# A first MLP product from three one-pass float32r products of 12-bit parts, in place of float32 half products of a seven-product scheme

## The chip, the cores and the metric

The kernel runs on one core of one Trainium2 chip. The time is device microseconds from the start to the end of one execution. The kernel before takes 355.83 us, the median of three runs (355.64 to 357.01). TensorE (PE) multiplies matrices and writes to PSUM; VectorE (DVE), ScalarE (ACT) and GpSimd (POOL) do the elementwise work; SyncE (SP) starts most of the transfers. Each engine has its own queue and works through it in the order of the program.

## What is computed

Two blocks follow each other. The first is a Mamba-2 state-space layer over 4 batches, 8 heads, 768 tokens, with heads 32 wide and a state of 16. The second is an MLP with a hard-swish on 3072 tokens of width 256, with 2048 hidden columns:

```
x = attn_out.transpose(0, 2, 1, 3).reshape(B * S, H * D)   # 3072 x 256
h = x @ w_in                                               # 256 -> 2048
relu6 = np.clip(h + 3.0, 0.0, 6.0)
g = h * relu6 / 6.0
return (g @ w_out).astype(np.float32)                      # 2048 -> 256
```

The weights arrive as float64, so the kernel decodes them to float32 from their bits.

## The kernel before

The sequence is cut into six chunks (`NC`) of 128 positions. A chunk holds 128 positions of all 4 batches, so 512 tokens (`TB`). For each chunk the state-space layer makes `yT`, which is 256 features (two tiles of 128, index `j`) by 512 tokens. The first MLP product turns it into 16 tiles `gT` (index `f`) of 128 hidden columns by 512 tokens, and the second MLP product turns those into the output. The program is software-pipelined by hand: the state-space work of chunk `c = k + 1` stands inside the second MLP product of chunk `k`, and loads stand one chunk further ahead. Nothing is reordered; the order in which the Python code emits instructions is the order in each engine's queue.

**Weights.** Each weight matrix comes in four parts (0 to 3 are `w_in`, 4 to 7 `w_out`), 1 MB each. `decode(i)` is a generator with five steps, and `weights(i, n)` takes n of them. Step 1: ACT copies the top 16 bits (L198). Step 2: DVE takes exponent, sign and high mantissa bits (L215, L217, L201). Step 3: ACT, first half of the exponent (L221). Step 4: ACT, second half (L223), and DVE the full mantissa (L205). Step 5: DVE joins sign and exponent (L228) and multiplies (L236), which finishes 128 x 1024 weights. The dictionary `weave` says after which `f` of chunk 0 each step is emitted. Parts 0 and 1 are decoded before chunk 0's MLP, parts 2 to 5 within its first product, 6 and 7 at the beginning of its second.

**First product, chunk 0.** `mlp_in(0, f)` multiplies in plain float32: two products of 128 x 128 weights by 512 tokens per `f` (L616), then `ramp` on ACT (L694: relu of h/6 + 1/2) and `times_ramp` on DVE (L699: the smaller of that and 1, times h). Its results go through four PSUM banks, f0 to f3.

**First product, chunks 1 to 5.** A seven-product scheme on 2 x 2 blocks of halves (features by token halves, hidden columns in even and odd tiles): for each pair `s` of hidden tiles, `lead`, `early`, `middle` and `last` issue seven products of 128 x 128 weights by 256 tokens (all at L658, in `half_product`), where a direct product would take eight. Its sums of weights are made once by `in_weight_sums` (L640), its sums of `yT` for each chunk by `sum_y` (L655, right after `keep`), and partial results are copied and added by ACT (L673, L680) and DVE (L674, L686, L687) between the products. `ramp` and `times_ramp` follow for each of the two tiles.

**Second product.** For chunk 0, `first_out` (L713): 128 products by four quarters `i` of the hidden columns and four batches `b`; quarter `i` needs part `4 + i` of the weights and the gT tiles 4i to 4i + 3. For chunks 1 to 4, `wide_units` (L836), and for chunk 5, `out_units` (L772), again in a seven-product scheme; POOL makes its sums of `gT` (`g_sums`, L758, four operations for every four tiles) and DVE its sums of weights (`weight_sums`, L740). The next chunk's `lead` for its first tiles is emitted near the end: before the last two products of `first_out`, or at unit 12 of `wide_units`.

**State-space work.** `scores`, `multiply`, `renew`, `mix` and `keep` (L527 to L608) for the next chunk stand inside the second product; `keep` copies the result into `yT` on ACT. `conceal` (POOL, L158), `decay` (ACT, L385) and `ends` (POOL, L396) prepare the chunk after that.

Of the kernel before, what the change touches and what calls it, by code (L numbers as in the profile page):

```python
# [8 lines left out]
FP32 = mybir.dt.float32  # L9
U32 = mybir.dt.uint32  # L10
# [10 lines left out]
def kernel(  # L21
# [34 lines left out]
    NQ = NH // 2  # L56
    HU = NH // 2
# [57 lines left out]
    def load_x(c):  # L115
        sl = slice(c * P, (c + 1) * P)
        xts[c] = loads.tile([P, NB * NH, D], FP32, name="xt")
        nc.sync.dma_start(out=xts[c], in_=x[:, :, sl, :].rearrange("b h s d -> s (b h) d"))

    w_in = const.tile([P, NK, DF], FP32, name="w_in")  # L120
    w_sum = const.tile([P, NF // 2, P], FP32, name="w_sum")
# [50 lines left out]
    nc.vector.memset(half, 0.5)  # L172
    bias_hi = const.tile([P, 1], FP32, name="bias_hi")
# [12 lines left out]

    def decode(i):
# [7 lines left out]
        s = att.tile([P, n], U16, name="ws")  # L195
        e = att.tile([P, n], U16, name="we")
# [33 lines left out]
        if i < NP:  # L230
            dst = w_in[:, :, i * FP * P:(i + 1) * FP * P]
            m, e = (t.rearrange("p (k f) -> p k f", k=NK) for t in (m, e))
        else:
            dst = w_out[:, (i - NP) * FP:(i - NP + 1) * FP, :]
            m, e = (t.rearrange("p (k f) -> p k f", k=FP) for t in (m, e))
# [8 lines left out]
    picks = const.tile([P, G * N], BF16, name="picks")  # L244
# [77 lines left out]

    yTs, states, mids, bTs, bss, tmps = {}, {}, {}, {}, {}, {}
# [67 lines left out]
    def ends(c, b):  # L391

        if b == 0:
            bss[c] = att.tile([P, G, N], FP32, name="bs")
        hs = slice(b * NH, b * NH + NH)
        nc.gpsimd.tensor_tensor(  # L396
            out=bss[c][:, hs], in0=Bs[c][:, hs],
            in1=Ls[c][:, b, :, HT - 1:HT].to_broadcast([P, NH, N]), op=ALU.mult)
# [174 lines left out]
    def renew(c):  # L573

        states[c] = att.tile([P, NB, 2 * D], FP32, name="state")
        later = att.tile([P, NB, 2 * D], FP32, name="later", bufs=1)
        nc.vector.tensor_tensor(
            out=later, in0=mids[c], in1=etos[c][:, :, P - 1:P].to_broadcast([P, NB, 2 * D]),
            op=ALU.mult)
        new_state(states[c], adds[c], later)  # L580
# [22 lines left out]
    def keep(c):  # L603

        yTs[c] = att.tile([P, NK, NB, P], FP32, name="yT")
# [7 lines left out]
    def mlp_in(k, f):  # L613
        h = ps.tile([P, NK, 2 * P], FP32, name="h", tag=f"f{f % 4}")
        for j in range(NK):
            nc.tensor.matmul(  # L616
                out=h.rearrange("p r i -> p (r i)"), lhsT=w_in[:, j, f * P:(f + 1) * P],
# [11 lines left out]
    wi = w_in.rearrange("p k (j e c) -> p k e j c", e=2, c=P)  # L629
    in_sums, y_sums, evens, odds, parts_of = {}, {}, {}, {}, {}  # L630

    def in_weight_sums():
        for h in range(2):
            js = slice(h * NJ // 2, (h + 1) * NJ // 2)
            a11, a12, a21, a22 = (wi[:, k, e, js] for e in range(2) for k in range(2))
            s1, s2 = (att.tile([P, NJ // 2, P], FP32, name="w_sum", tag=t) for t in ("ws", "we"))
            s4 = w_sum[:, js]
            for o, p_, q_, op in ((s1, a21, a22, ALU.add), (s2, s1, a11, ALU.subtract),
                                  (s4, a12, s2, ALU.subtract), (a21, a11, a21, ALU.subtract)):
                nc.vector.tensor_tensor(out=o, in0=p_, in1=q_, op=op)  # L640
            for n, t in ((1, s1), (2, s2), (3, a21), (4, s4)):
                in_sums.setdefault(n, []).extend(t[:, i] for i in range(NJ // 2))
            yield

    def y_half(k, j, r):
        return yTs[k][:, j, 2 * r:2 * r + 2].rearrange("p b i -> p (b i)")

    def sum_y(k):
        ts = att.tile([P, 3, 2 * P], FP32, name="ts", bufs=1)
        t1, t2, t4 = (ts[:, i] for i in range(3))  # L650
        t3 = y_half(k, 0, 1)
        y_sums[k] = {1: t1, 2: t2, 3: t3, 4: t4}
        for o, p_, q_ in ((t1, t3, y_half(k, 0, 0)), (t3, y_half(k, 1, 1), t3),
                          (t2, y_half(k, 1, 1), t1), (t4, y_half(k, 1, 0), t2)):
            nc.vector.tensor_tensor(out=o, in0=p_, in1=q_, op=ALU.subtract)  # L655

    def half_product(bank, r, lhsT, rhs, start=False):
        nc.tensor.matmul(  # L658
            out=bank[:, r], lhsT=lhsT, rhs=rhs, start=start, stop=True, skip_group_check=True)

    def lead(k, s):

        (pool, tag), (pool_e, tag_e) = (
            ((ps, "f0"), (ps, "f2")), ((ps, "f1"), (ps, "f3")),
            ((ps_y, "y0"), (ps_y, "y1")))[s % 3]
        odds[k, s] = odd = pool.tile([P, 2, 2 * P], FP32, name="odd", tag=tag)
        evens[k, s] = even = pool_e.tile([P, 2, 2 * P], FP32, name="even", tag=tag_e)
        parts_of[k, s] = up = ffn.tile([P, 2, 2 * P], FP32, name="up", bufs=2)  # L670
        half_product(odd, 1, wi[:, 0, 0, s], y_half(k, 0, 0), start=True)
        half_product(odd, 0, in_sums[3][s], y_sums[k][3])
        nc.scalar.copy(out=even, in_=odd[:, 1:2].to_broadcast([P, 2, 2 * P]))  # L673
        nc.vector.tensor_copy(out=up[:, 1], in_=odd[:, 0])  # L674

    def early(k, s):
        even = evens[k, s]
        half_product(even, 0, wi[:, 1, 0, s], y_half(k, 1, 0))
        half_product(even, 1, in_sums[2][s], y_sums[k][2])
        nc.scalar.copy(out=parts_of[k, s][:, 0], in_=even[:, 1])  # L680

    def middle(k, s):
        even, odd, up = evens[k, s], odds[k, s], parts_of[k, s]
        half_product(odd, 0, wi[:, 1, 1, s], y_sums[k][4])
        half_product(even, 1, in_sums[1][s], y_sums[k][1])
        nc.vector.tensor_tensor(out=odd[:, 0], in0=odd[:, 0], in1=up[:, 0], op=ALU.add)  # L686
        nc.vector.tensor_tensor(out=odd[:, 1], in0=even[:, 1], in1=up[:, 1], op=ALU.add)  # L687

    def last(k, s):
        half_product(evens[k, s], 1, in_sums[4][s], y_half(k, 1, 1))  # L690
# [12 lines left out]
    def first_out(b, i, c):  # L703
# [6 lines left out]
        for f in range(i * FP, (i + 1) * FP):  # L710
            if b == NB - 1 and f == NF - 2:
                lead(c, 0)
            nc.tensor.matmul(  # L713
                out=o[:, b % 2], lhsT=gTs[0][:, f, b * P:(b + 1) * P], rhs=w_out[:, f],
                start=(f == 0 and b % 2 == 0), stop=True, skip_group_check=True)
        if i == NP - 1 and b % 2:
            ob = ffn.tile([P, 2, DM], FP32, name="ob", bufs=2)
# [11 lines left out]
    def weight_sums():  # L729


        t3 = const.tile([P, NJ, P], FP32, name="t3")
# [27 lines left out]
    def out_units(k):  # L760
# [15 lines left out]
        for t in range(2):  # L776
# [9 lines left out]
            if t == 0:  # L786
                unit(oa, 0, quarter(0, 0, 0), w4[:, 0, 0], rest)
                unit(oa, 3, quarter(0, 0, 1), w4[:, 0, 0], rest)
                x1 = ffn.tile([P, 2, P], FP32, name="x1")
# [6 lines left out]
            res = ffn.tile([P, 5, P], FP32, name="res", bufs=2)  # L796
# [7 lines left out]
            u = ffn.tile([P, 2, P], FP32, name="u", bufs=2)  # L804
# [108 lines left out]
    def results(c, parts=range(2)):  # L913
        mix(c, parts)
        keep(c)
        sum_y(c)
# [4 lines left out]

    def load(c):
        load_bc(c)
        load_x(c)
# [60 lines left out]
    load(1)  # L985


    weave = {}
    for i in range(2, NP + 2):
        for j in range(5):  # L990
            weave.setdefault(4 * i - 8 + j, []).append(i)
    weave[NF - 1].append(NP + 2)
    for k in range(NC):
        gTs[k] = ffn.tile([P, NF, TB], FP32, name="gT")
        c, ahead = k + 1, k + 2
        if k == 0:
            for f in range(NF):
                mlp_in(k, f)
                for i in weave.get(f, []):
                    weights(i, 1)  # L1000
                if f in (6, 8):
                    diff_exp(c, f // 2 - 3)
            load(ahead)
# [3 lines left out]
            sums, sums_in = weight_sums(), in_weight_sums()  # L1007
            for i in range(NP):
                for b in range(NB):
                    first_out(b, i, c)  # L1010
                    if (i, b) == (0, 0):
                        weights(NP + 3, 1)
                        weights(NP + 2, 1)
                        weights(NP + 3, 3)
                        rows(ahead)
                    elif (i, b) == (1, 0):
                        next(sums_in)
                        next(sums_in)
# [16 lines left out]
                    elif (i, b) == (3, 1):  # L1035
                        results(c)
                        next(sums)
                        decay_ends(ahead, 3)
                    elif (i, b) == (3, 3):
# [3 lines left out]
        for s in range(NJ):  # L1043
            early(k, s)
            if s == 0:
                if ahead < NC:
                    load(ahead)
                if c < NC:
                    carry(c)
            if s < NJ - 1:  # L1050
                lead(k, s + 1)
            if s:
                last(k, s - 1)
                ramp(k, 2 * s - 2, evens[k, s - 1])
            middle(k, s)
            if s:
                times_ramp(k, 2 * s - 2, evens[k, s - 1])
            ramp(k, 2 * s + 1, odds[k, s])
            times_ramp(k, 2 * s + 1, odds[k, s])
            if s in (1, 3) and ahead < NC:  # L1060
                conceal(ahead, s // 2)
            if s in (3, 5) and c < TURN:
                turn(c, s // 4)
            if s in (2, 4, 6):
                g_sums(k, s - 2)
        for i, _ in enumerate((wide_units if c < NC else out_units)(k)):
            if i == 0:
                s = NJ - 1
                last(k, s)
                ramp(k, 2 * s, evens[k, s])  # L1070
                times_ramp(k, 2 * s, evens[k, s])
                g_sums(k, s - 1)
                if k == 1:
                    next(sums)
            if c < NC:
# [11 lines left out]
                if i == (7 if c == TURN else 6):  # L1087
                    results(c, (1,) if c == TURN else range(2))
                    if ahead < NC:
                        from_start(ahead)  # L1090
# [4 lines left out]
                if i == 12:  # L1095
                    lead(c, 0)

# [29 lines left out]
```

## Time and profile before

| view | value |
|---|---|
| median of the runs shown | 355.83 us |
| the profiled execution's span | 353.6 us |
| first product of chunk 0 on PE (L616) | 22.8 to 50.3 us, 64 records |
| second product of chunk 0, with the state-space work of chunk 1 | 50.3 to 83.0 us |
| chunk 1 (from its first `lead` to the next chunk's) | 83.0 to 137.5 us |
| chunks 2, 3, 4 | 53.9, 53.6 and 54.0 us |
| chunk 5 | 299.0 to 353.6 us |
| DVE multiply that finishes weight parts 2, 3, 4, 5, 6, 7 (L236), start | 33.84, 41.34, 48.35, 54.76, 60.68, 63.68 us |

The profile covers one execution. "Busy" counts the time in which an engine has at least one instruction; PE records overlap, since matmuls are pipelined, so the distance from start to start is the time that one costs in a stream. A float32 product of 128 x 128 weights leaves two MATMUL records and two weight-load records. "PEclk" is the clock granted to TensorE.

### The profile page before, as it was taken

What the parts mean: (1) busy time and instruction counts of PE and PEld (TensorE: products, weight loads), DVE (VectorE), ACT (ScalarE), POOL (GpSimd) and SP (SyncE); (2) the same over time, 40 slices, a digit from 0 to 9 for tenths busy, and PEclk for the clock granted to TensorE, in tenths of its full rate; (3) what the DMA queues carried; (4) which work ended last, traced back from release to release, by engine and by line L of the source; (5) the groups of instructions that cost most, each with busy time, mean ns of one, the idle gap of its engine ahead of it and who ended that gap; (6) DMA issues with size and microseconds to landing.
All of it is one profiled execution on the core that took longest, in us unless ns stands there. A gap on an engine that the chain in (4) does not pass through costs nothing.

```text
span 353.6 us, 8557 instructions
## 1 busy us (share of the span) xinstructions
PE 343.7 (97%) x3488; PEld 281.9 (80%) x3488; DVE 227.4 (64%) x426; ACT 178.7 (51%) x394; POOL 138.0 (39%) x139
## 2 busy tenths in 40 slices
PE   6699999999999999999999999999999999999996
PEld 2454458888887888888888888888888888888996
DVE  6689999975797437786437787436687322688111
ACT  4768887258764741665641575551575011466100
POOL 3300000362498621099612099710078600068700
PEclk9999999999999999999999999999999999999999
DMA  8999969502925052256034256001200001200000
GB/s 168 178 335 162 272 157 122 128 2 78 164 55 66 4 125 51 35 70 81 2 72 97 36 67 91 4 4 18 34 9 1 4 3 20 34 8 2 0 32 30
DMA packets 91607, 24.92 MB, mean 70 GB/s; under 512 B 84208, under 2 KB 87952, under 8 KB 91056
## 3 DMA queue, kind: packets, MB, share of 16 engines
q1 hardware_dynamic: 87184, 23.06, 35.7%
q10 hardware_dynamic: 4384, 1.31, 1.7%
q8 instruction: 27, 0.44, 0.5%
q14 instruction: 12, 0.10, 0.1%
HBM read 21.07 MB, written 3.29 MB: 69 GB/s over the span
## 4 chain that ended last, share of the span: by engine, by line
PE 91%; DVE 3%; DMA 3%; ACT 1%; SPq 1%; issue 1%; DVEq 0%; ACTq 0%
PE even L658 18%; PE odd L658 13%; PE wb L836 12%; PE wc L836 8%; PE o L713 8%; PE h L616 8%; PE wa L836 8%; PE oa L772 4%; PE ob L772 4%; PE y L594 3%; PE y L500 2%; PE cb L527 2%; DMA raw<-in_moe_w_in_dram 2%; PE y L539 1%; DMA pairs<-in_C_dram 1%; SPq L100 1%
## 5 line engine op out<-in xcount | busy, mean ns | idle before, releaser
L758 POOL TENSOR_TENSOR s<-gT 128x512 f32<-128x512 f32 x20 | 26.3, 1317 | 86.0 <-DVE gT L699 86.0
L658 PE MATMUL even<-ts,w_sum 128*128 128x256 f32 x160 | 48.2, 383 | 0.0
L694 ACT ACTIVATE gT<-odd,half 128x512 f32<-128x512 f32 x40 | 27.5, 688 | 34.9 <-DVE odd L687 34.9
L658 PE MATMUL odd<-yT,w_in 128*128 128x256 f32 x160 | 41.1, 379 | 0.0
L673 ACT COPY even<-odd 128x512 f32<-128x512 f32 x40 | 23.0, 576 | 27.7 <-PE odd L658 25.5
L658 PEld LDWEIGHTS even<-ts,w_sum 128*128 128x128 f32 x160 | 29.9, 190 | 5.3 <-ACT up L680 1.5
L699 DVE SCALAR_TENSOR_TENSOR gT<-gT,odd 128x512 f32<-128x512 f32 x40 | 27.5, 688 | 9.9 <-ACT gT L694 9.9
L658 PEld LDWEIGHTS odd<-yT,w_in 128*128 128x128 f32 x160 | 30.4, 190 | 4.1
L385 ACT ACTIVATE L<-L,cum_n 128x64 f32<-128x64 f32 x128 | 31.5, 340 | 0.0
L836 PE MATMUL wb<-s,w_out 128*128 128x256 f32 x128 | 30.7, 382 | 0.0
L694 ACT ACTIVATE gT<-even,half 128x512 f32<-128x512 f32 x40 | 27.8, 695 | 4.4 <-PE even L658 4.4
L699 DVE SCALAR_TENSOR_TENSOR gT<-gT,even 128x512 f32<-128x512 f32 x40 | 27.2, 679 | 4.4 <-ACT gT L694 4.4
L713 PE MATMUL o<-w_out,gT 128*128 128x256 f32 x128 | 28.7, 381 | 0.0
L616 PE MATMUL h<-yT,w_in 128*128 128x512 f32 x64 | 27.7, 594 | 0.0
L674 DVE COPY up<-odd 128x256 f32<-128x256 f32 x40 | 16.9, 423 | 15.8 <-ACT even L673 15.1
L713 PEld LDWEIGHTS o<-w_out,gT 128*128 128x128 f32 x128 | 24.1, 190 | 3.7 <-issue 0.5
L403 POOL TENSOR_TENSOR tmp<-state,eto 128x256 f32<-128x256 f32 x5 | 3.4, 684 | 60.4 <-DMA eto<-cum_e 51.1
L836 PEld LDWEIGHTS wb<-s,w_out 128*128 128x128 f32 x128 | 24.0, 190 | 3.4
L758 POOL TENSOR_TENSOR s<-s,gT 128x512 f32<-128x512 f32 x20 | 25.5, 1273 | 1.6
L758 POOL TENSOR_TENSOR gT<-gT 128x512 f32<-128x512 f32 x20 | 25.4, 1272 | 0.0
L758 POOL TENSOR_TENSOR s<-gT,s 128x512 f32<-128x512 f32 x20 | 25.4, 1270 | 0.0
L658 PE MATMUL even<-yT,w_sum 128*128 128x256 f32 x80 | 24.4, 387 | 0.2
(150 smaller groups left out, 657.9 us busy)
## 6 DMA issues: line engine op xcount, KB each, us to landing
raw<-in_moe_w_out_dram SPq DMA_DIRECT2D x4, 1024.0 KB
L<-cum_d SPq DMA_DIRECT2D x8, 512.0 KB
xt<-in_x_dram SPq DMA_DIRECT2D x6, 512.0 KB
raw<-in_moe_w_in_dram SPq DMA_DIRECT2D x3, 1024.0 KB
out_dram<-back SPq DMA_DIRECT2D x128, 16.0 KB
eto<-cum_e SPq DMA_DIRECT2D x20, 64.0 KB
B<-in_B_dram SPq DMA_DIRECT2D x5, 256.0 KB
raw<-in_moe_w_in_dram ACTq DMA_DIRECT2D x1, 1024.0 KB
```

Source lines behind the costliest of these rows:

```text
L385: nc.scalar.activation(Ls[c][:, b, h], Ls[c][:, b, h], AF.Exp, bias=cum_n[:, c, g:g + 1])
L594: nc.tensor.matmul(out=ys[c][a, u][d0:d0 + D, b], lhsT=xt[rows, b * NH + h], rhs=Ls[c][rows, b, h], start=(b == 0 and a >= min(c, 1)), sto ...
L616: nc.tensor.matmul(out=h.rearrange("p r i -> p (r i)"), lhsT=w_in[:, j, f * P:(f + 1) * P], rhs=yTs[k][:, j].rearrange("p b i -> p (b i)") ...
L658: nc.tensor.matmul(out=bank[:, r], lhsT=lhsT, rhs=rhs, start=start, stop=True, skip_group_check=True)
L673: nc.scalar.copy(out=even, in_=odd[:, 1:2].to_broadcast([P, 2, 2 * P]))
L674: nc.vector.tensor_copy(out=up[:, 1], in_=odd[:, 0])
L694: nc.scalar.activation(gTs[k][:, f], h.rearrange("p r i -> p (r i)"), AF.Relu, bias=half, scale=1.0 / 6.0)
L699: nc.vector.scalar_tensor_tensor(out=g, in0=g, scalar=1.0, in1=h.rearrange("p r i -> p (r i)"), op0=ALU.min, op1=ALU.mult)
L713: nc.tensor.matmul(out=o[:, b % 2], lhsT=gTs[0][:, f, b * P:(b + 1) * P], rhs=w_out[:, f], start=(f == 0 and b % 2 == 0), stop=True, skip_ ...
L758: nc.gpsimd.tensor_tensor(out=o, in0=p_, in1=q_, op=op)
L772: nc.tensor.matmul(out=bank[:, slot], lhsT=lhs[:, j], rhs=rhs[:, j], start=(clear and j == 0), stop=True, skip_group_check=True)
L836: nc.tensor.matmul(out=bank[:, slot], lhsT=lhs[:, j], rhs=rhs[:, j], start=(clear and j == 0), stop=True, skip_group_check=True)
```

## The change

`w_in` is no longer kept as one float32 tensor. Each weight and each element of `yT` is split into a high part (the value times 1 - 2^-13, rounded to the 12 significant bits of float32r by the write), and a low part (what is left, which the weights' split scales by 2^12), and a third array `gap` holds the difference of the two scaled parts. The product is then (gap x gap), scaled in PSUM by -2^-12/(1 + 2^-12), plus high x high, plus low x low: three products of float32r operands, each of 128 x 128 weights by 512 tokens and over two feature tiles, so six matmuls for each hidden tile. The factor 1 + 2^-12 that remains is taken up by the constants of the activation (`half_up`, `UP`).

- `lead(k, f)` issues the two gap matmuls and the scaling of the PSUM bank (ACT for even `f` and for all of chunk 0, DVE for odd `f` otherwise); `follow(k, f)` issues the other four matmuls, the relu on ACT and the multiply on DVE. `lead` runs two tiles ahead, over six banks.
- `split_y(k)` splits `yT` (one ACT and two DVE operations of 128 x 1024); it stands in `results` where `sum_y` stood, and for chunk 0 ahead of `mlp_in(0, 2)`.
- `split_w(i)` splits weight part i in three steps (ACT and POOL; ACT; DVE or POOL), placed by `part`.
- In chunk 0 the tiles 0 to 7 still go through `mlp_in` in float32, tiles 8 to 15 through `lead` and `follow`. Parts 0 and 1 of `w_in` are decoded into float32 scratch tiles, parts 2 and 3 in place. The steps of parts 2 and 3 now fall on f = 0 to 3 and 4 to 7.
- `in_weight_sums`, `sum_y`, `half_product`, `early`, `middle` and `last` are gone.
- To make room in SBUF, `xt` and `bs` have one buffer instead of two, and `load_x` of the chunk ahead moves from the head of the first product to behind `results`; scratch tiles share buffers (`later`, `x1`, `u`, `ob`, `res`, `picks`, `t3`).

```diff
+    w_high, w_low, w_gap = (
+        const.tile([P, NK, DF], FP32R, name=n) for n in ("w_high", "w_low", "w_gap"))
...
+    highs, lows, gaps, hs = {}, {}, {}, {}
+
+    def split_w(i, engine):
+
+        w = first_in[i]
+        high, low, gap = (t[:, :, i * FP * P:(i + 1) * FP * P] for t in (w_high, w_low, w_gap))
+        nc.scalar.mul(high, w, CUT)
+        nc.gpsimd.tensor_tensor(out=low, in0=w, in1=high, op=ALU.subtract)
+        yield
+        nc.scalar.mul(low, low, 1.0 / Z)
+        yield
+        engine.tensor_tensor(out=gap, in0=high, in1=low, op=ALU.subtract)
+        yield
+
+    def split_y(k):
+
+        y = yTs[k].rearrange("p k b i -> p (k b i)")
+        high, low = (att.tile([P, NK * TB], FP32R, name=n, tag="y", bufs=3) for n in ("high", "low"))
+        nc.scalar.mul(high, y, CUT)
+        nc.vector.tensor_tensor(out=low, in0=y, in1=high, op=ALU.subtract)
+        gap = att.tile([P, NK * TB], FP32R, name="gap", **Y_GAP[min(k, 1)])
+        nc.vector.scalar_tensor_tensor(
+            out=gap, in0=low, scalar=-1.0 / Z, in1=high, op0=ALU.mult, op1=ALU.add)
...
+    def in_product(h, w, y, f, start=False):
+        for j in range(NK):
+            nc.tensor.matmul(
+                out=h, lhsT=w[:, j, f * P:(f + 1) * P], rhs=y[:, j],
+                start=(start and j == 0), stop=True, skip_group_check=True)
+
+    def lead(k, f):
...
+        pool, tag = ((ps, "f0"), (ps, "f1"), (ps, "f2"), (ps, "f3"), (ps_y, "y0"),
+                     (ps_y, "y1"))[f % 6]
+        hs[k, f] = h = pool.tile([P, TB], FP32, name="h3", tag=tag)
+        in_product(h, w_gap, gaps[k], f, start=True)
+        if k and f % 2:
+            nc.vector.tensor_scalar(
+                out=h, in0=h, scalar1=-Z / UP, scalar2=None, op0=ALU.mult)
+        else:
+            nc.scalar.mul(h, h, -Z / UP)
+
+    def follow(k, f):
+        h = hs.pop((k, f))
+        in_product(h, w_high, highs[k], f)
+        in_product(h, w_low, lows[k], f)
+        g = gTs[k][:, f]
+        nc.scalar.activation(g, h, AF.Relu, bias=half_up, scale=UP * UP / 6.0)
+        nc.vector.scalar_tensor_tensor(
+            out=g, in0=g, scalar=UP, in1=h, op0=ALU.min, op1=ALU.mult)
...
+    weave = {f: [] for f in range(NF)}
+    for f in range(NF // 2):
+        weave[f].append(2 + f // FP)
+    for f in (3, 7):
+        weave[f].append(2 + f // FP)
+    for i in range(NP, NP + 2):
         for j in range(5):
-            weave.setdefault(4 * i - 8 + j, []).append(i)
+            weave[min(4 * i - 8 + j, NF - 1)].append(i)
     weave[NF - 1].append(NP + 2)
+    splits = [split_w(i, nc.vector if i > 1 else nc.gpsimd) for i in range(NP)]
+    part = {1: (), 3: (2,), 5: (2,), 6: (2,), 7: (3,), 8: (3,), 9: (3,), 12: (0,), 14: (0, 1), 15: (1,)}
...
             for f in range(NF):
-                mlp_in(k, f)
-                for i in weave.get(f, []):
+                if f == 2:
+                    split_y(0)
+                if f < NF // 2:
+                    mlp_in(k, f)
+                else:
+                    if f < NF - 2:
+                        lead(k, f + 2)
+                    follow(k, f)
+                for i in weave[f]:
                     weights(i, 1)
+                for i in part.get(f, ()):
+                    next(splits[i])
+                if f in (6, 7):
+                    lead(k, f + 2)
                 if f in (6, 8):
                     diff_exp(c, f // 2 - 3)
...
+        for f in range(NF):
...
+            if f + 2 < NF:
+                lead(k, f + 2)
+            follow(k, f)
```

## The prediction, on record before the changed kernel ran

> **What bounds the kernel now.** I read the busy table by slices first, then the chain that ended last, then the windows by stage, then the groups.
>
> ```profile
> span 353.6 us, 8557 instructions
> ...
> PE   6699999999999999999999999999999999999996
> ...
> DVE  6689999975797437786437787436687322688111
> ```
>
> PE is full from the third slice to the last but one. DVE is as full in slices 4 to 8 (27 to 71 us), and there alone: chunk 0, where it decodes weights.
>
> ```profile
> PE 91%; DVE 3%; DMA 3%; ACT 1%; SPq 1%; issue 1%; DVEq 0%; ACTq 0%
> ```
>
> ```profile
> core 0: us, PE busy (x) PEld busy (x) DVE busy (x) ACT busy (x) POOL busy (x), PEclk, DMA share, GB/s
> 22.80:50.30 27.50, 27.50 (x66) 12.22 (x65) 25.40 (x39) 23.41 (x30) 0.00 (x0) 1.00 0.93 200
> 50.30:83.00 32.70, 32.70 (x454) 28.43 (x453) 27.99 (x43) 20.27 (x47) 9.53 (x12) 1.00 0.67 99
> 83.00:137.50 54.50, 54.33 (x549) 45.83 (x549) 36.54 (x70) 30.24 (x80) 31.66 (x29) 1.00 0.46 81
> 137.50:191.40 53.90, 53.90 (x545) 46.01 (x545) 33.36 (x65) 27.61 (x72) 26.72 (x25) 1.00 0.36 59
> ```
>
> From chunk 1 on, PE alone sets the pace (DVE 33 of 54 us). In chunk 0's first product PE never waits, but DVE is busy 25.4 of 27.5 us and ACT 23.4: the cover is thin there.
>
> ```profile
> L658 PE MATMUL odd<-yT,w_in 128*128 128x256 f32 x160 | 41.1, 379 | 0.0
> L616 PE MATMUL h<-yT,w_in 128*128 128x512 f32 x64 | 27.7, 594 | 0.0
> L699 DVE SCALAR_TENSOR_TENSOR gT<-gT,h 128x512 f32<-128x512 f32 x16 | 10.8, 682 | 1.0 <-ACT gT L694 0.6
> L758 POOL TENSOR_TENSOR s<-gT 128x512 f32<-128x512 f32 x20 | 26.3, 1317 | 86.0 <-DVE gT L699 86.0
> L221 ACT ACTIVATE we<-we,bias_hi 128x1024 bf16<-128x1024 uint16 x8 | 9.2, 1149 | 3.1 <-DVE we L215 3.0
> L740 DVE TENSOR_TENSOR t<-w_out 128x1024 f32<-128x1024 f32 x1 | 1.2, 1219 | 0.0
> L348 PE MATMUL d<-less,split 128*128 128x512 bf16 x8 | 2.4, 382 | 0.9 <-DVE split L280 0.9
> ```
>
> **Price of a product.** L616: 32 float32 products in 27.66 us of the chain, 0.864 us each. L658 with half the columns: 0.432. No float32r stands in the trace. The one-pass row is L348 (bf16): its pair at 7.47 us ends after 0.60 us, one lasts 0.38, so the second starts 0.22 later, a quarter of 0.864. Bounds for a float32r product of 512 tokens: 0.216 below, 0.864 (no gain over float32) above. I take 0.216: the operands are four bytes wide, but L616 streams such operands too. A weight load lies between 97 ns (bf16, L348) and 190 (float32, L658), and either is hidden behind products 216 ns apart, as the 190 are now behind records 216 ns apart.
> The Trainium skill (FP8 and Floating Point Precision, TensorE Precision Notes) gives true float32 four passes and says reduced-precision float32 is read as four bytes and truncated; a single pass would be 0.216 by that, too, though it states no rate.
>
> **Chunks 1 to 5: a gain.** Removed: 56 x 0.432 = 24.2 us of PE per chunk. Added: 96 x 0.216 = 20.7. Gain 3.46 us a chunk, 17.3 in all, if PE still sets the pace. ACT loses L673 and L680 (8 x 0.94) and gains 8 scalings (0.58, by L673): it has 16 x 0.69 + 8 x 0.58 = 15.7 us of work; DVE 24 x 0.69 = 16.5; both under 20.7. A scaling has the other tiles' 2.6 us before its bank's follow needs it; on DVE it queues behind one multiply, and is ready some 0.8 us early. In chunk 1 turn puts 2.1 us of DVE work in between: about 1.3 us of wait, where before this chunk lost about 0.8. POOL's sums take 4 x 5.1 us for a stage of 20.7, so they end about 9 us after it (before: at 172.7, 9.4 after the stage's 163.3), and their first reader on PE comes 13 us after it. In chunks 2 to 5 split_y (0.37 x 4 copies, then 1.15 + 1.22 + 1.23 us) ends about 5 us after mix, lead comes 9 to 10 us after it (126.9 and 137.5 in chunk 1): hidden by wide_units; without that cover it costs 3.6 a chunk. Moved load_x: its queue, SP, now waits for mix, and the rows and 32 stores queue behind it; its reader (L539 of the next chunk) is some 40 us later. Shared buffers, bs and the memset of half_up: nothing, by the same distances.
>
> **Chunk 0: a loss.** The rule of the walk: each engine takes its queue in order; DVE multiply 0.61 from start to start, mantissa/exponent step 1.40, L205 1.14, L228 0.72, L236 1.15; ACT 0.58 and 1.05 to 1.15; POOL 128 x 1024 as two L758, 2.5 (the lower bound too; the upper is 4.0, by eight L396 of 0.50).
>
> ```profile
> 31.39 1.22 DVE L205 SCALAR_TENSOR_TENSOR wm<-raw,wm 128x1024 f32<-128x1024 uint32 x1
> 32.52 0.68 DVE L699 SCALAR_TENSOR_TENSOR gT<-gT,h 128x512 f32<-128x512 f32 x1
> 33.12 0.69 DVE L228 TENSOR_TENSOR we<-we,ws 128x1024 uint16<-128x1024 uint16 x1
> 33.84 1.23 DVE L236 SCALAR_TENSOR_TENSOR w_in<-wm,we 128x1024 f32<-128x1024 f32 x1
> ```
>
> Part 2 is finished here at 35.1. (1) split_y(0) puts 2.4 us ahead of it, one multiply falls behind it (-0.6): 36.8. (2) high 1.15 on ACT, low 2.5 on POOL, scaling 1.15 on ACT; tile 6's relu, which queues behind that scaling, and its multiply, 1.3; gap 1.2 on DVE: 44.1. (3) lead(0, 8) reads that gap, and mlp_in(0, 7) stands behind it on PE, which finished tile 6 at 22.83 + 7 x 1.728 = 34.9. PE waits 9.2 us. (4) Tile 7 runs 44.6 to 46.3, its relu and multiply to 47.8, then part 3's L205, L228, L236 to 50.8. The same chain again (high 52.0, low 54.5, scaling 55.7; on ACT a decay exponential, a lead's scaling and tile 9's relu; on DVE its multiply, part 4's 1.40 and the gap): 60.6. lead(0, 12) starts at 60.7; PE ran out at 53.4, and waits 7.3 us. (5) The last tiles follow ACT, from 62.1 on: three relus of 0.58, three lead scalings of 0.50, L221 1.13, and L223, L198 and the high of part 0 at 1.05, 7.5 us in all; then follow(0, 15), 0.86: 70.6, where first_out starts, against 50.33 before. That is +20.3, with the 3.46 us of cheaper products in it. (6) The second quarter of first_out needs part 5. On ACT, L221, a low and a high stand ahead of tile 15's relu (74.7), its multiply ends at 76.0, then L205, L228 and L236 at 79.0, 1.6 us after the first quarter (70.6 + 6.9): +21.8. Parts 6 and 7 follow by 4.4 us each, a quarter by 6.9: no more waits. in_weight_sums (8 x 0.79 of DVE) is gone there, but PE has no wait in this stage before: nothing. (7) The end: before, lead(1, 0) started at 82.98, 0.8 us after the last yT copy. Now high, low and gap (1.15 + 1.22 + 1.23) follow that copy: 82.19 + 21.8 + 3.6 = 107.6. Chunk 0 costs +24.6.
>
> (8) The clock: at the start of the trace the 128 x 512 bf16 matmuls of L336 start 0.43 us apart (weight loads at 2.51, 2.93, 3.36) until 5.5 us, at 7.47 us 0.22 apart. If PE comes back at half pace after the 9.2 us wait, lead(0, 8) and tile 7 (2.16 us) take 2.2 more, on the path. Bounds: 0 (the granted clock stays at 1.00 even at the start) and 5.1 (three waits, 1.7 each). I take 2.2.
> The Trainium skill (TensorE: Matmul & The Clock Gate, What's actually happening) speaks against this change here: after about 3.4 us idle PE runs at half clock until it was busy for about as long. By that rule it would be an estimated +4 and a median of 367, by the granted-clock column 0 and 363.
>
> **Sum**, on the profiled execution: 353.6 - 17.3 + 24.6 + 2.2 = 363.1 span. The median lies 2.2 above that execution's span before: 365.3, rounded 365.
>
> **The rivals.**
> A, faster: the splits don't hold PE, because parts 2 and 3 are ready by tile 6 and 10. Then chunk 0 gains 3.5: 353.6 - 17.3 - 3.5 + 2.2 = 335. For it: PE sets 91% of the chain. Against: L236 at 33.84 with DVE already 4 us behind PE, and four dependent operations behind it. It decides if chunk 0 loses less than 15.5 us. 0.08.
> B, no change: chunk 0 loses 15.5 to 19, as when tiles 7 and 9 get through ACT and DVE earlier than walked: 354 to 357.6. 0.07.
> C: float32r doesn't run in one pass but at the pace of one float32 record of 512 columns, 0.432: 96 x 0.432 = 41.5 a chunk, 353.6 + 5 x 17.3 + 27 + 2.2 = 469. For it: no float32r row. 0.05.
> D: my walk, with POOL at 4.0 (+1.5 in each of the two chains) and three slow restarts (+2.9), and one more wait at each chunk's head: 371 to 380. 0.10.
> Forecast: 358 to 371, 0.70.
>
> Within 0.5% (354.05 to 357.6) is what a measurement of this kernel can't tell from no change. Faster 0.08, same 0.07, slower 0.85. The range 356 to 373 leaves out A, most of B, C and part of D.
>
> **What would show it.** Chunk 0: PE idle before lead(0, 8) and lead(0, 12), 9 and 7 us, released by DVE's gap; first_out at 70; lead(1, 0) at about 108, released by DVE. Chunks 1 to 4: 50.2 us from lead to lead instead of 53.9, in_product records 216 ns apart, no idle PE. It would be wrong if those records stood further apart, or if PE had no wait before 60 us.

## The result, and the profile after

| | before | after |
|---|---|---|
| median | 356.37 us (4 runs, 355.64 to 357.01) | 385.64 us (4 runs, 384.73 to 387.1) |
| ratio after/before | | 1.083, 95% interval 1.080 to 1.086 |
| profiled execution's span | 353.6 us | 385.3 us |
| lead(1, 0) starts | 82.98 us | 123.40 us |
| from there to the end | 270.6 us | 261.9 us |

The change makes the kernel slower by 29.3 us. The forecast was 365, slower by 9: the sign was right, the size was not. The last two rows split it. Chunk 0 costs 40.4 us more (forecast 24.6, and 2.2 for the clock), and chunks 1 to 5 give back 8.7 (forecast 17.3).

The first view is the head of the page after: busy tenths and granted clock in 40 slices of 9.6 us, then the chain's shares by engine.

```profile
span 385.3 us, 8266 instructions
...
PE   6799182874996999999999999998999999999996
...
DVE  6668634579456575558764196742667633467111
...
PEclk9859757895999999999999999999999999999999
...
PE 77%; DVE 10%; ACT 8%; DMA 2%; issue 1%; SPq 1%; DVEq 0%
```

PE was full from the third slice on; now it has holes in slices 5 to 10 and in 13, and DVE and ACT hold 18% of the chain, where they held 4%. The clock, 9 throughout before, falls as low as 5 in the first ten. From slice 14 on nothing of that is left.

The next view is PE's timeline after, start, duration, operation, and in brackets the idle time before it with its releaser. Only the rows with an idle time over 2 us in chunk 0 are shown.

```profile
47.26 1.22 PE L670 MATMUL h<-gap,w_gap 128*128 128x512 f32 x2 [8.02 <-DVE w_gap L653]
...
65.85 1.22 PE L670 MATMUL h<-gap,w_gap 128*128 128x512 f32 x2 [6.70 <-DVE w_gap L653]
...
91.59 11.89 PE L721 MATMUL o<-w_out,gT 128*128 128x256 f32 x40 [7.18 <-DVE w_out L248]
...
123.40 0.93 PE L670 MATMUL h<-gap,w_gap 128*128 128x512 f32 x3 [2.97 <-DVE gap L663]
```

The first two are the waits of the forecast (9.2 and 7.3 us, released by DVE's gap of parts 2 and 3), and so is the fourth (the split of y). The third was forecast at 1.6 us; the wait for part 5, which the second quarter of `first_out` needs, is 5.6 us longer than walked.

The windows by stage, with the columns of the prediction's windows (busy time of PE, PEld, DVE, ACT and POOL, then the granted clock):

```profile
24.50:77.30 52.80, 34.49 (x84) 19.18 (x81) 28.53 (x38) 33.29 (x44) 6.19 (x3) 0.76 0.44 98
77.30:123.40 46.10, 35.95 (x454) 30.12 (x452) 30.61 (x36) 25.17 (x56) 18.27 (x17) 0.89 0.39 65
...
175.40:227.35 51.95, 51.95 (x530) 43.02 (x529) 30.86 (x50) 26.77 (x65) 26.35 (x24) 1.00 0.33 54
```

In chunk 2 PE is busy all the time, for 51.95 us, where before it was 53.90 and the forecast said 50.2. So the loops lose to no wait; the products themselves are dearer. PE's timeline there shows it (each row is two products):

```profile
178.74 0.63 PE L670 MATMUL h<-high,w_high 128*128 128x512 f32 x2
179.21 0.63 PE L670 MATMUL h<-low,w_low 128*128 128x512 f32 x2
179.67 0.63 PE L670 MATMUL h<-gap,w_gap 128*128 128x512 f32 x2
```

Rows start 0.467 us apart, so a float32r product of 512 columns costs 0.233 us, not 0.216. The chain has the same in one line, 92 products in 21.50 us:

```profile
178.44 21.50 PE h L670 x92
```

What delays part 5 is seen on DVE, and on POOL beside it:

```profile
83.20 2.32 DVE L213 SCALAR_TENSOR_TENSOR wm<-raw,wm 128x1024 f32<-128x1024 uint32 x1
85.44 2.83 DVE L236 TENSOR_TENSOR wse<-wse 128x1024 uint16<-128x1024 uint16 x1
88.30 3.25 DVE L248 SCALAR_TENSOR_TENSOR w_out<-wm,wse 128x1024 f32<-128x1024 f32 x1
```

```profile
82.06 2.37 POOL L649 TENSOR_TENSOR w_low<-w,w_high 128x1024 fp32r<-128x1024 f32 x1 [3.44 <-ACT w_high L648]
84.39 6.07 POOL L653 TENSOR_TENSOR w_gap<-w_high,w_low 128x1024 fp32r<-128x1024 f32 x2
```

Before, the same three DVE operations took 1.22, 0.69 and 1.23 us. Here each ends only after a POOL operation has ended: L213 at 85.52, 1.1 after POOL's low (84.43); L248 at 91.55, 1.1 after POOL's second gap (90.46). The order alternates: the two gaps of POOL last 3.32 and 2.79 us, and the second one's end less a low's 2.37 is 88.1, about where L236 ends (88.27). The two engines take turns, one whole instruction at a time.

The Trainium skill (SBUF — State Buffer, SBUF: two separate sides) states such a rule: POOL and those DVE operations that read two operands from SBUF, or run in a two-port mode, share a pair of ports, as an exclusive lock for a whole instruction. The trace agrees, 2.83 us for 0.69; and the multiply L694, which reads one operand from SBUF and one from PSUM, keeps its 0.69 at 76.89 while a low runs on POOL (75.85 to 78.62). L223, which reads one operand from SBUF, lost time beside that low too, 1.42 us at 77.49 for 0.41 at 91.46; whether it runs in that mode no run here shows. The prediction drew on no such rule: its walk gave POOL's work its own price, and put at nothing what that work costs the DVE operations beside it.

### The profile page after: what moved, and what is told of

It is laid out like the page before. It is cut to its first block, busy times and chain, and to the rows that moved or that the text cites. A ratio compares the mean times of both kernels' runs of the same rounds, so it can differ in the third digit from the quotient of the medians.

```text
span 385.3 us, 8266 instructions
## 1 busy us (share of the span) xinstructions
PE 345.9 (90%) x3424; PEld 277.3 (72%) x3424; DVE 219.1 (57%) x333; ACT 187.1 (49%) x376; POOL 154.9 (40%) x145
## 4 chain that ended last, share of the span: by engine, by line
PE 77%; DVE 10%; ACT 8%; DMA 2%; issue 1%; SPq 1%; DVEq 0%
PE h L670 29%; PE wb L847 11%; PE wc L847 7%; PE wa L847 7%; PE o L721 5%; PE oa L780 3%; PE ob L780 3%; PE h L629 2%; PE y L607 2%; PE y L513 2%; PE cb L540 2%; DMA raw<-in_moe_w_in_dram 1%; ACT L L398 1%; ACT gT L693 1%; DVE wm L213 1%
## 5 line engine op out<-in xcount | busy, mean ns | idle before, releaser
L694 DVE SCALAR_TENSOR_TENSOR gT<-gT,h 128x512 f32<-128x512 f32 x88 | 60.4, 688 | 47.0 <-ACT gT L693 44.1
L693 ACT ACTIVATE gT<-h,half_up 128x512 f32<-128x512 f32 x88 | 60.5, 689 | 37.3 <-PE h L670 37.3
L670 PE MATMUL h<-gap,w_gap 128*128 128x512 f32 x176 | 58.9, 422 | 19.2 <-DVE w_gap L653 14.7
L670 PE MATMUL h<-high,w_high 128*128 128x512 f32 x176 | 57.1, 406 | 2.4 <-ACT h L686 2.1
L670 PE MATMUL h<-low,w_low 128*128 128x512 f32 x176 | 56.1, 400 | 0.0
L670 PEld LDWEIGHTS h<-gap,w_gap 128*128 128x128 f32 x176 | 33.9, 196 | 29.7 <-DVE w_gap L653 16.0
L686 ACT ACTIVATE h<-h 128x512 f32<-128x512 f32 x48 | 28.1, 587 | 37.9 <-PE h L670 35.8
L670 PEld LDWEIGHTS h<-high,w_high 128*128 128x128 f32 x176 | 33.3, 193 | 12.4 <-ACT h L686 3.0
L670 PEld LDWEIGHTS h<-low,w_low 128*128 128x128 f32 x176 | 33.8, 192 | 8.3
L683 DVE TENSOR_SCALAR h<-h 128x512 f32<-128x512 f32 x40 | 27.7, 692 | 1.1 <-PE h L670 1.0
```

The source lines that it names most:

```text
L670: nc.tensor.matmul(out=h, lhsT=w[:, j, f * P:(f + 1) * P], rhs=y[:, j], start=(start and j == 0), stop=True, skip_group_check=True)
L683: nc.vector.tensor_scalar(out=h, in0=h, scalar1=-Z / UP, scalar2=None, op0=ALU.mult)
L686: nc.scalar.mul(h, h, -Z / UP)
L693: nc.scalar.activation(g, h, AF.Relu, bias=half_up, scale=UP * UP / 6.0)
L694: nc.vector.scalar_tensor_tensor(out=g, in0=g, scalar=UP, in1=h, op0=ALU.min, op1=ALU.mult)
```

## The experiments

Three theories stand for what the forecast missed. **Contention**: POOL's splits hold up DVE's decoding. **Clock**: after each wait PE comes back at half pace, more often than once. **Rate**: a float32r product costs 0.233 us, and more needs to be known of why. The rival to the first two is that the walk through ACT and DVE was wrong, to the third that the loops wait for something. Runs 1 to 5 and 8 to 10 are one execution each, and the kernel before, timed again beside them, took 354.96 to 360.1 us; so what is read are starts and durations in the traces, and totals only where they differ by more than that.

**Run 1, the gaps of parts 0 and 1 on DVE.**

```diff
-    splits = [split_w(i, nc.vector if i > 1 else nc.gpsimd) for i in range(NP)]
+    splits = [split_w(i, nc.vector) for i in range(NP)]
```

> The gap step of weight parts 0 and 1 goes from POOL to DVE; nothing else changes. Theory (POOL and DVE slow each other on SBUF operands): in the changed kernel part 5's L213, L236 and L248 take 2.3, 2.8 and 3.3 us while POOL runs the two gaps, against 1.2, 0.7 and 1.2 elsewhere; without them they fall back to 1.2 to 2.3, 0.7 and 1.2, PE's wait for part 5 falls from 7.2 us to 2 to 4, and the span by 4 to 9 us, to 376 to 381. Rival (the wait comes from what is queued ahead of part 5 on ACT and DVE, and POOL has no part in it): the wait stays at 7 us, the span at 385, or 2.4 more.

377.93 us, span 376.0. DVE's timeline:

```profile
79.64 2.32 DVE L213 SCALAR_TENSOR_TENSOR wm<-raw,wm 128x1024 f32<-128x1024 uint32 x1
81.89 0.68 DVE L236 TENSOR_TENSOR wse<-wse 128x1024 uint16<-128x1024 uint16 x1
82.60 1.23 DVE L248 SCALAR_TENSOR_TENSOR w_out<-wm,wse 128x1024 f32<-128x1024 f32 x1
```

and PE's:

```profile
83.88 8.90 PE L721 MATMUL o<-w_out,gT 128*128 128x256 f32 x40 [3.03 <-DVE w_out L248]
```

L236 and L248 are back at 0.68 and 1.23. L213 still takes 2.32: its POOL neighbour, the low at 78.51, was left. PE's wait for part 5 falls from 7.18 to 3.03 us, and the second quarter starts 10.1 us after `first_out` instead of 14.25. lead(1, 0) starts at 112.69. More work on DVE, and the stage is shorter: contention, not DVE's load. About 1.8 us more come from the clock, since the second quarter's 40 records take 8.90 us behind the shorter wait (10.68 in run 10 below).

**Run 2, 256 columns a product.** The same float32r operands, two products of 256 tokens for one of 512.

```diff
+            for r in range(2):
+                rs = slice(r * 2 * P, (r + 1) * 2 * P)
-                out=h, lhsT=w[:, j, f * P:(f + 1) * P], rhs=y[:, j],
-                start=(start and j == 0), stop=True, skip_group_check=True)
+                    out=h[:, rs], lhsT=w[:, j, f * P:(f + 1) * P], rhs=y[:, j, rs],
+                    start=(start and j == 0 and r == 0), stop=True, skip_group_check=True)
```

> Each float32r product of 512 tokens is issued as two of 256, all else equal; the matmul starts of the chunk loops are read (0.233 us apart in the changed kernel, for 512 tokens). Theory L (the weight load sets the pace): still 0.233 apart, so 0.467 for 512 tokens, a loop of 44.8 us in place of 22.4, span near 500. Theory F (a fixed cost of about 18 ns on top of 0.216): 0.126 apart, a loop of 24.2, span near 394. Theory C (the columns stream more slowly): 0.117 apart, loop and span unchanged at 22.4 and 385.

382.67 us, span 380.9. The chain's stretch of a loop:

```profile
174.75 21.75 PE h L672 x184
```

That is 0.118 us for 256 columns, against 0.233 for 512 (21.50 us for 92). With twice the weight loads (192 ns each) the loop is 1% longer (21.75 us for 21.50). So neither the weight load nor a fixed cost of 18 ns a product makes the price; it goes with the columns, 0.456 ns each, where a pass of a plain float32 product costs 0.864/4/512 = 0.422 ns.

**Run 3, tile 7 ahead of lead(0, 8).** In the changed kernel `lead(0, 8)` stands ahead of `mlp_in(0, 7)` on PE, although the tile could run.

```diff
-                if f in (6, 7):
-                    lead(k, f + 2)
+                if f == 7:
+                    lead(k, 8)
+                    lead(k, 9)
```

> lead(0, 8) moves from before tile 7's float32 products to behind them; nothing else. Theory (PE's order holds tile 7, and with it part 3's decode on DVE, behind the gap): tile 7 runs at about 39 instead of 48.3 us, DVE goes from part 2's gap straight to tile 7's multiply and part 3, about 5 us earlier, lead(0, 12) starts at 58 to 62 instead of 65.9, the span falls by 4 to 8 us. Rival (the chain of part 3 is bound by DVE and ACT alone): lead(0, 12) stays at 65 to 66 and the span within 1.5 us of 385.

381.54 us, span 379.6. lead(0, 8) starts at 43.76 as in the other runs, lead(0, 12) at 58.89, first_out at 70.77, lead(1, 0) at 115.78: the last three are some 3 us earlier than in run 10 below. The order on PE costs 3 us, less than the 4 to 8 us of span that were expected (3.1 against run 10). The first wait, 7.01 us, is shorter only because tile 7 now runs before it; the second is 5.03 us.

**Run 4, the waits filled.** While it would wait, PE makes products that nothing reads: 8, 7 and 8 float32 products (`busy`) into a free bank, ahead of lead(0, 8), lead(0, 12) and the second quarter of `first_out`.

```diff
+                    if f == 10:
+                        busy(7, ps.tile([P, NB * P], FP32, name="fill", tag="f0"))
...
+                if f == 6:
+                    busy(8, ps_y.tile([P, NB * P], FP32, name="fill", tag="y1"))
...
+                    if (i, b) == (1, 0):
+                        busy(8, ps.tile([P, NB * P], FP32, name="fill", tag="f0"))
```

> Float32 products of the identity (8, 7 and 8 of 0.864 us) go into unused banks on PE in the three waits of chunk 0: before lead(0, 8), lead(0, 12) and the second quarter of first_out. Theory (the waits lower TensorE's clock, and the slow restarts are on the path): the granted clock stays at 1.00 from 31 to 110 us, lead(0, 8) with tile 7 takes 2.2 us instead of 4.6, the first 20 us after the second quarter's start lose nothing (3 us in the changed kernel), and the span falls by 5 to 10 us. Rival (the clock is not on the path, or does not fall): the span stays within 1.5 us of 385.

376.23 us, span 374.4, mean clock 1.00. PE's timeline:

```profile
43.95 0.73 PE L670 MATMUL h<-gap,w_gap 128*128 128x512 f32 x2 [1.90 <-DVE w_gap L653]
44.52 1.88 PE L629 MATMUL h<-yT,w 128*128 128x512 f32 x4
...
60.45 0.71 PE L670 MATMUL h<-gap,w_gap 128*128 128x512 f32 x2 [0.78 <-DVE w_gap L653]
...
70.60 7.07 PE L721 MATMUL o<-w_out,gT 128*128 128x256 f32 x32
...
84.88 8.90 PE L721 MATMUL o<-w_out,gT 128*128 128x256 f32 x40 [0.34 <-DVE w_out L248]
```

More work on PE, and the kernel is faster. At full clock the walk of the forecast comes out within 0.3 us: it had 44.1, 60.7 and 70.6 for the starts of the two leads and of `first_out`. Its inner steps fit as well (DVE finishes part 2 at 36.74 for 36.8, part 3 at 50.84 for 50.8), so this is no luck, and the rival, that the walk was wrong, falls up to there. The second quarter (forecast 79.1) is run 1's matter: its distance to `first_out` is 14.3 us here as in the changed kernel.

**Run 5, bf16 in place of float32r.** The parts are rounded to fewer bits; only times are read. (That float32r keeps 12 bits is what the kernel's constants assume; no run here measures it.)

```diff
-FP32R = mybir.dt.float32r
+FP32R = mybir.dt.bfloat16
```

> The parts high, low and gap are stored as bf16 in place of float32r; everything else stands, so the numbers in them are cut to 8 bits and only times are read. If the 0.233 us of a product belongs to the four-byte operands of float32r, the products of chunks 2 to 5 stand 0.216 us apart and the stretch of 92 products in the chain falls from 21.50 to about 19.9. If any one-pass product of 512 columns needs 0.233 in this loop (the read of the operands beside DVE and ACT, or the PSUM banks), it stays at 21.5.

374.37 us, span 372.5.

```profile
172.47 19.97 PE h L670 x92
```

19.97 us for 21.50, so 1.5 us less for 92 products, or 0.217 us each for 0.234, in the same loop, beside the same ACT and DVE work on the banks and into the same banks. The 0.233 is float32r's own. Whether it comes from the width of the moving operand or from the kind of multiplication wasn't separated.

**Runs 6 and 7, chunk 0 back in plain float32.** All 16 tiles of chunk 0 go through `mlp_in`, decoding returns to the order of before, and the splits of all four parts stand in the second product of chunk 0, on ACT and DVE, with the last two gaps on POOL at the head of chunk 1; `split_y(0)` is gone. Run 7 also puts `results(1)` one block earlier (the last lines of the diff).

```diff
-                if f < NF // 2:
-                    mlp_in(k, f)
-                else:
-                    if f < NF - 2:
-                        lead(k, f + 2)
-                    follow(k, f)
+                mlp_in(k, f)
...
+                        split_step(0, 1, 2, 3)
                         rows(ahead)
+                    elif (i, b) == (1, 0):
+                        split_step(0, 1, 2, 3)
...
+                        split_step(0, 1, 2, 3)
+                        split_step(0, 1)
...
                     elif (i, b) == (3, 0):
                         next(sums)
+                        results(c)
                         decay_ends(ahead, 2)
                     elif (i, b) == (3, 1):
-                        results(c)
```

> Chunk 0 goes back to plain float32 for all 16 tiles; the weights are split during its second product, 13 operations on ACT, DVE and none on POOL until chunk 1, and split_y(0) is gone. If the loss sits in chunk 0's splits alone, the first product ends near 50.3 as before, lead(1, 0) starts near 86.6 (82.98 plus the 3.6 of high, low and gap of y), and the rest takes 261.5 as in the runs so far: a span near 348, faster than the kernel before by about 1.5%. If the splits cost the same wherever they stand, because ACT or DVE runs out in the second product, lead(1, 0) is past 95 and the span past 356.

> As the run with chunk 0 in plain float32, with mix, keep and the split of y for chunk 1 one block (1.7 us) earlier in the second product. If the 3.6 us of the split stand on the path, lead(1, 0) comes 1.5 to 2 us earlier than in that run and the span is near 346; if mix then has to wait for the decays on ACT or DVE, nothing is gained.

Run 6: 352.52 us (4 runs, 351.82 to 353.49), ratio to before 0.991 (0.987 to 0.994). Run 7: 349.71 us (347.61 to 352.19), ratio 0.982 (0.975 to 0.989). Both are far below the changed kernel. Both intervals lie below 1, so both beat the kernel before, run 6 by 1%; whether run 7 gains 2% its interval leaves open. PE's timeline of run 7:

```profile
23.34 29.43 PE L628 MATMUL h<-yT,w 128*128 128x512 f32 x64
52.61 15.70 PE L722 MATMUL o<-w_out,gT 128*128 128x256 f32 x72
...
86.47 1.17 PE L671 MATMUL h<-gap,w_gap 128*128 128x512 f32 x4 [1.00 <-DVE gap L664]
```

The first product takes 29.4 us (27.7 in run 6; here the granted clock is 0.50 between 24 and 26 us), `first_out` follows it with no wait, and lead(1, 0) starts at 86.47, 3.5 later than before. Counted from `first_out`, that is 33.86 us for run 6's 36.38: the earlier `results` gains 2.5, for 1.5 to 2 expected. From there to the end it is 262.3 us, as in the changed kernel. So the loops' gain of 8.3 is real, and the four splits of the weights need not cost what they cost in the changed kernel. That it was the place alone isn't shown: these runs also take most of the splits off POOL, keep all of chunk 0 in float32 and drop a split of y. Run 6 missed its 348 by 3.8 in span: PE waits 3.73 us for the split of y and restarts at half clock (four lead products last 2.04 us instead of 1.17), and chunk 4 has 1.7 us of issue time in it (time in which PE waited for nothing that the profile shows).

**Runs 8 and 9, runs 1 and 4 together.** Run 8 is both edits; run 9 also cuts the third filling from 8 products to 3.

```diff
-                        busy(8, ps.tile([P, NB * P], FP32, name="fill", tag="f0"))
+                        busy(3, ps.tile([P, NB * P], FP32, name="fill", tag="f0"))
```

> The gaps of parts 0 and 1 on DVE, and the three waits of PE filled with products that nothing reads, together. Alone the one took 7.1 us and the other 6.1 us off the start of lead(1, 0), which stood at 119.8. If these are two separate causes, they add up: lead(1, 0) near 106.6, where the forecast had 107.6 with one slow restart in 2.2 more, and a span near 368. If the slow clock only mattered since it delayed the same chain as the contention, lead(1, 0) stays at 110 or later.

> As the run with both, but the last filling is cut from 8 products to 3, since with the gaps on DVE part 5 is ready 10.1 us after first_out starts (3.0 us of wait) and 8 products held PE some 4 us beyond that. If contention and clock are two separate causes: first_out near 70.6, its second quarter near 80.7, lead(1, 0) near 109.5 and a span near 371 in an execution without a slow start. If they are not, lead(1, 0) stays at 112 or later.

Run 8: 382.48 us, lead(1, 0) at 118.57; run 9: 377.75 us, span 375.8, lead(1, 0) at 112.32. Neither reached its number. Run 8's third filling was sized for a wait of 7 us that run 1's edit had cut to 3: DVE finishes part 5 at 84.52, and PE is held until 89.88. Its first 28 records of L629 also took 15.15 us, 2.8 more than in run 10. In run 9 the clock was not held:

```profile
54.64 7.73 PE L503 MATMUL fill<-ident 128*128 128x512 f32 x14
...
71.56 1.22 PE L670 MATMUL h<-high,w_high 128*128 128x512 f32 x2 [1.85 <-ACT h L686]
73.44 7.76 PE L721 MATMUL o<-w_out,gT 128*128 128x256 f32 x32
```

The filling itself ran slowly (run 4: 6.17 us for the same 14 records), and so did `first_out`'s start, 7.76 for 7.07. The second quarter starts 10.2 us after `first_out`, but not for part 5, which is ready at 82.63; the third filling held PE until 83.61. Runs 4 and 9 have the same short waits of 1.5 to 2.0 us left; in run 9 the clock came down around them and in run 4 it did not. By the letter of the expectations both runs fall on the side of the rival, lead(1, 0) past 110 and past 112, but with the fillings in the way they test it badly. That the two causes add up in one run is not shown; each is shown by its own stage.

**Run 10, the changed kernel again, unchanged.**

> The changed kernel once more, unchanged. If the half clock between 18 and 31 us of its profiled execution comes and goes from one execution to the next, L629 runs its 28 records in 12.3 us here, and lead(1, 0) starts near 119.8 as in the run with 256 columns; if it belongs to this kernel, it is there again and lead(1, 0) is near 123.4.

384.61 us, span 382.7. PE's timeline:

```profile
44.01 1.22 PE L670 MATMUL h<-gap,w_gap 128*128 128x512 f32 x2 [8.73 <-DVE w_gap L653]
45.03 3.10 PE L629 MATMUL h<-yT,w 128*128 128x512 f32 x4
...
62.10 1.22 PE L670 MATMUL h<-gap,w_gap 128*128 128x512 f32 x2 [5.90 <-DVE w_gap L653]
...
88.23 10.68 PE L721 MATMUL o<-w_out,gT 128*128 128x256 f32 x40 [7.18 <-DVE w_out L248]
...
118.81 1.74 PE L670 MATMUL h<-gap,w_gap 128*128 128x512 f32 x4 [2.90 <-DVE gap L663]
```

L629's first 28 records take 12.33 us (14.68 in the profile shown above), and lead(1, 0) starts at 118.81, so the half clock between 16 and 28 us in that profile comes and goes from one execution to the next; runs 5, 7 and 8 had some of it too (down to 0.50 or 0.54 in parts of 22 to 30 us). This execution is the one to hold against the forecast's terms.

## Why the prediction was right in sign and wrong in size

Forecast 365 us with a range of 356 to 373, measured 385.64. The sign was right, and for the forecast's reason: PE waits in chunk 0 for the chain of splits. Three terms were too small: the price of a product, the clock of step (8), and in step (6) the cost of POOL's work to DVE, which stood at nothing.

Starts in us, of the forecast (without its 2.2 us for the clock) and of run 10:

| | forecast | run 10 | step that failed |
|---|---|---|---|
| lead(0, 8) | 44.1 | 44.01 | |
| lead(0, 12) | 60.7 | 62.10 | clock (8) |
| first_out | 70.6 | 73.98 | clock (8) |
| its second quarter | 79.1 | 88.23 | contention, step (6) |
| lead(1, 0) | 107.6 | 118.81 | clock (8) |
| from there to the end | 253.3 | 263.9 | price of a product; clock; issue time |

- **Steps (1) to (5)**, the walk through ACT, DVE and POOL up to `first_out`, held: with the clock at 1.00, in run 4, its three starts came out within 0.3 us. Its premise, PE idle behind a chain of dependent splits, is what decides the sign. In the chains of parts 2 and 3 POOL's low ran while DVE had no operation with two SBUF operands, so the missing price did not show there.
- **Step (6)** failed, and its size is 5.75 us (14.25 from `first_out` to its second quarter, for 8.5). The walk priced L205, L228 and L236 by their lone durations, with POOL's gaps of parts 0 and 1 running beside them. Run 1 showed 4.15 of it (14.25 to 10.10); of the rest 1.1 is L213 beside POOL's low (2.32 for 1.22), still there in that run, and the other 0.5 was not followed up.
- **Step (7)**, the split of y on the path, held: 28.8 us from the second quarter to lead(1, 0) in runs 1 and 4, for 28.5.
- **Step (8)**, the clock, was mis-sized: the forecast took one slow restart, 2.2 us, and PE restarts slowly after each of its three long waits. In run 10 that cost 3.4 up to `first_out` (run 4: 70.60), about half of it behind each of the first two waits, and 1.8 in the second quarter (40 records in 10.68 us; run 1: 8.90), 5.2 in all, where the forecast's upper bound, 1.7 for each of three waits, had 5.1. Another 1.6 comes behind lead(1, 0), where the clock is 0.91 between 110 and 130 us (from lead(1, 0) to its first `follow` 3.96 us; run 4: 2.34). In run 10 the granted clock is 0.60 between 39 and 47 us, 0.50 between 59 and 66, and 0.76 between 78 and 92. The Trainium skill (TensorE: Matmul & The Clock Gate, What's actually happening) ties the half clock to an idle window of about 3.4 us, and calls the window free-running. The three long waits, 5.9 to 8.7 us, agree. Other rows don't follow from that alone: in run 10 PE also falls to half pace at 54.20, after a wait of 1.98 us, run 1 keeps the full clock after 3.03 us, and in the first profile of the changed kernel the clock is 0.50 from 16 to 28 us although PE is busy all the time from 18 us on.
- **The price of a product** was mis-sized: 0.216 taken, 0.233 measured, 0.0174 x 96 = 1.67 us a chunk and 8.3 in all, half of the gain. Run 4, with the clock at 1.00, has 260.7 us from lead(1, 0) to the end: 253.3 and 8.3, less the 1.0 of the next point. The price was read off a bf16 row, with the reason that float32 streams four-byte operands at that pace. Run 5 showed that the bf16 row prices bf16. The Trainium skill (FP8 and Floating Point Precision, TensorE Precision Notes) gives true float32 four passes, and L616's 0.864 is four times 0.216; but a product of float32r, which the prediction took for one such pass, costs 0.233.
- **ACT, DVE and POOL in chunks 1 to 5** hide as forecast: PE is busy 51.95 of 51.95 us in chunk 2. In chunk 1 `turn` costs 0.3 us of wait, where the forecast had 1.3.
- **The sum.** In run 10's span of 382.7 the forecast's 363.1 is off by 19.6: 8.3 of rate, 5.75 of contention, 4.6 of clock beyond the 2.2, 0.3 of step (7) and some 1.6 of issue time in chunk 3 (53.5 us for 51.9; its cause is open), less the 1.0 of `turn`. The execution profiled first needs 4.6 us more up to lead(1, 0), 3.25 of it before lead(0, 8), and 2.0 less from there to the end.
- **The rivals.** A and B fall: part 2 and 3 were late as walked. C falls: 0.233 is far from 0.432. D was the nearest, 371 to 380 with three slow restarts and a POOL operation at 4.0 us, but its mechanism was another: POOL's operations cost 2.4 where nothing held them, and what they cost DVE was left out.

## What to carry to other kernels

A walk through engines' queues that prices each operation by its lone duration needs one more column: what runs on POOL at that time, since a DVE operation with two SBUF operands cost up to 2.1 us more here beside a POOL operation of 2.4. A long wait of PE (5.9 to 8.7 us here) costs its length and then some 1.7 us at half pace; work put into it can save the second part (5.1 us up to lead(1, 0) in run 4), but not in every execution (run 9). Where a preparation (here the splits) serves five of six chunks, try keeping the first chunk in the old form and preparing behind it: here that turned 8% slower into 1 to 2% faster.

## What the runs showed of the hardware that was not expected

- A float32r product of 128 x 128 weights and 512 columns costs 0.233 us, 8% more than a bf16 product or one pass of a float32 product (0.216), and 0.118 with 256 columns.
- POOL and DVE took turns by whole instructions: a DVE operation of 0.69 us lasted 2.83, and a POOL gap 3.32, where POOL's low of the same size took 2.37.
- The granted clock can fall to 0.50 in the first 30 us, in executions of kernels that did not show it in another execution (run 10 against the profile after), at a cost of 0.7 to 2.8 us in L629's first 28 records (12.33 us without it; 13.05 in run 5, 14.68 in the profile after, 15.15 in run 8). What brings it down there stays open.
